# Layer 2 of a three-stage kernel: two operands of the activation put into PSUM, block sums read from SBUF, every transfer issued by one queue, loads issued earlier

## The chip, the cores and the metric

The kernel runs on one core of a Trainium2 chip. The metric is device microseconds of one execution, from repeated timed runs; a separate profiled execution gives the trace. The engines are named as in the profile: PE (matmuls), PEld (its weight loads), DVE (VectorE), ACT (ScalarE), POOL (GpSimd) and SP, which here only issues transfers. A name with a q at its end (ACTq, SPq) is the engine's sequencer.

## The reference, cut to what matters

An attention stage feeds a first two-matrix layer, and that one a second. All the changed code is in the second layer. With 1792 tokens, width 768 and inner width 2048:

```python
h = x @ w_in                                   # 1792x768 @ 768x2048
P = a[0] + a[1]*h + a[2]*h**2 + a[3]*h**3
Q = 1.0 + abs(b[0])*abs(h) + abs(b[1])*h**2
g = P / (Q + 1e-06)
out = g @ w_out                                # 1792x2048 @ 2048x768
```

## The kernel before, in words

**Precision.** Every matmul operand is split into a high and a low part, and a product is three matmuls (high by high, high by low, low by high). `split`, `split2`, `split_x` and `split_g2` are such splits: ACT casts the high part, and DVE (POOL where `nc.gpsimd` is named) subtracts it for the low part.

**Layer 2, first product.** The tokens are cut into four blocks of 512, 384, 512 and 384, taken in the order 0, 2, 1, 3. For each block there are 8 turns, so 32 turns `n` in all (`HN`). `first2(n)` runs 36 matmuls on PE and leaves two banks of h side by side, in one of the three PSUM tiles `hps` (turn 0 uses the two banks `hb`). So in turns 0 to 15 a step of the activation has 2 x 512 = 1024 elements for each partition, and in turns 16 to 31 it has 2 x 384 = 768.

**The activation.** `act_step(n)` does `act_a(n)` and then `act_b(n-1)`, one turn late. In `act_a`, ACT makes |h| (L733), b1|h|+b0 (L734) and a3 h + a2 (L736); POOL multiplies the second by the first, which gives q (L737); DVE builds the numerator u in two steps (L739, L741), and the second of them is the last reader of the `hps` tile, so that PE may use it for turn n+3. In `act_b`, ACT takes the logarithm of q + 1 (L750) and the exponential of its negative (L751), which is a first value r of 1/Q. DVE then makes (q+1) r (L752), (u+a0) r (L753) and the Newton product, ((q+1) r - 2) u (L754). All tensors of these three steps lie in SBUF, in tiles of one large buffer `sb`, handed out by two rings: `us` with four tiles for u, `aq` with six for |h|, q and r.

**Block sums.** The second product is a seven-product block scheme (two halves of the tokens by two halves of the inner width). It wants g's blocks "11", "12", "22" and four sums S1 to S4. `g_out(n)` stores a turn's g to the DRAM tensor `gk`. Once the four blocks of one place are there, `gs_load` loads them all again, POOL makes four sums (`gs_sums`, L818), and `gs_out` stores the four sums. Ten of the sixteen groups of sums are made in turns 15 to 31, and six during the second product. `wt_load`, `wt_sums` (POOL, L790) and `wt_out` do the like for w_out, in turns 5 to 12.

**Layer 2, second product.** `second2(u)` runs 112 units of 12 matmuls (9 for the narrower part), 1176 matmuls in all. Unit `u` needs g split (`split_g2(u)`) and every other unit a new piece of w_out split (`split_w2(v)`); `load_g2` and `load_w2` fetch them ahead. `evict` empties the banks (`obank`).

**Queues.** The program is written out in order, and each engine runs its own instructions in that order. A transfer whose data or buffer isn't ready holds back whatever stands behind it in the queue of the engine that issues it. Stores of g, and loads and stores of g's sums, are issued by ACT here, between its activations; so are the first eight loads of w_out (L864). The other transfers are issued by SP.

Of the kernel before, what the change touches and what calls it, by code (L numbers as in the profile page):

```python
# [11 lines left out]
F32 = mybir.dt.float32  # L12
# [29 lines left out]
def attention_moe_moe(ctx: ExitStack, tc: tile.TileContext, q, k, v, w_in1, w_out1, w_in2, w_out2, a, b2, out):  # L42
# [699 lines left out]

    gst = {}

    def act_b(n):
# [12 lines left out]
        gst[n] = (gk[p][:, at_ : at_ + 2, c0 : c0 + w], u_, u)  # L758
# [16 lines left out]

    def wt_load(kk):
        wsum[kk] = [wif.get(), wif.get()]
        for t, c in zip(wsum[kk], (kk, kk + HF)):
            nc.sync.dma_start(out=t, in_=wd[1][c]["o"])

    def wt_sums(kk):
        t, u = wsum[kk]
        b11, b12, b21, b22 = t[:, :HM], t[:, HM:], u[:, :HM], u[:, HM:]
        for o, i0, i1, op in (
            (b22, b22, b12, ALU.subtract),
            (b12, b12, b11, ALU.subtract),
            (b11, b22, b11, ALU.add),
            (b21, b11, b21, ALU.subtract),
        ):
            nc.gpsimd.tensor_tensor(out=o, in0=i0, in1=i1, op=op)  # L790

    def wt_out(kk):
        for i, t in enumerate(wsum[kk]):
            nc.sync.dma_start(out=wt[kk][i], in_=t)
            wif.put(t)

    hf = Ring([])
    gsum = {}

    def halves(part, kk):  # L800
        w = blocks[part][1]
        return [t[:, : 2 * w].rearrange("p (k t) -> p k t", k=2) for t in gsum[part, kk]]

    def gs_load(part, kk):
        c0, w = blocks[part]
        gsum[part, kk] = (hf.get(), hf.get())
        for i, t in enumerate(halves(part, kk)):
            nc.scalar.dma_start(out=t, in_=gk[kk][:, 2 * i : 2 * i + 2, c0 : c0 + w])

    def gs_sums(part, kk):  # L810
        g22, g21, g11, g12 = (t[:, i] for t in halves(part, kk) for i in range(2))
# [8 lines left out]
    def gs_out(part, kk):  # L820
        c0, w = blocks[part]
        for i, t in enumerate(halves(part, kk)):
            nc.scalar.dma_start(out=gk[kk][:, 4 + 2 * i : 6 + 2 * i, c0 : c0 + w], in_=t)
        hf.put(*gsum.pop((part, kk)))

# [119 lines left out]
    with tc.manual_schedule():  # L945
# [3 lines left out]

        hb.extend(fixed("hb", 2, [P, 512], F32, hb_p))  # L950
        pairs.put(*fixed("pair", 3, [P, 2, 512], F32, ps_p))
# [276 lines left out]
        def temps(w):  # L1228
            tm = [sb[:, i * 2 * w : (i + 1) * 2 * w] for i in range(10)]
            order_ = (0, 1, 2, 7, 8, 9, 3, 4, 5, 6) if w == BK else range(10)  # L1230
            tm = [tm[i] for i in order_]
            for ring, ts in ((us, tm[:4]), (aq, tm[4:])):
# [3 lines left out]
        temps(BK)
        SB2 = 20 * (BK - P)
        WTS = range(5, 13)
        GSUMS = {n: i for i, n in enumerate((15, 18, 20, 21, 23, 24, 26, 27, 29, 31))}
        GSUMS2 = {5 + 8 * i: 10 + i for i in range(6)}  # L1240
        GS = [(part, kk) for part in range(2) for kk in range(HF)]
        wt_held = []
        spare = []

        for n in range(HN):
            g, p = turn(n)
            nxt = turn(n + HF)[0] if n + HF < HN else None
            for kk in wt_held:
                wt_out(kk)
            wt_held.clear()  # L1250
            if n < 5:
# [3 lines left out]
                load_wi(2 * n + 12)  # L1255
            if n + 1 in WTS:
                wt_load(n + 1 - WTS[0])
            if n == WTS[-1] + 1:
                hf.put(*(wif_all[:, i * 2 * BK : (i + 1) * 2 * BK] for i in range(3)))
            if n == 2 * HF:  # L1260
                temps(BK - P)
            if n == 2 * HF + 3:
                hf.put(*(sb[:, SB2 + i * 2 * BK : SB2 + (i + 1) * 2 * BK] for i in range(3)))
            if nxt is not None and p in (3, 4, 5):
# [48 lines left out]
        obank.extend([*hb, *(hps[i % 3][:, j, :] for i in (1, 2, 0) for j in range(2))])  # L1313
        for u in range(NU):
            split_g2(u + 6)
            if u == 0:
                for i in range(9, 12):
                    load_g2(i)
            load_g2(u + 12)
            if u % 2 == 0:  # L1320
                load_w2(u // 2 + HF)
                if u >= 4:
                    split_w2(u // 2 + HF - 2)
            second2(u)
            if u == 1:
                act_step(HN)
            if u in (3, 6):
                g_out(HN - 3 + u // 3)
            if u == 2:
                gs_out(*GS[GSUMS[HN - 1]])  # L1330
                hf.free.clear()
                hf.put(*(wif_all[:, i * 2 * BK : (i + 1) * 2 * BK] for i in (2, 0, 1)))
                hf.put(sb[:, SB2 + 4 * BK : SB2 + 6 * BK])
            if u - 5 in GSUMS2:
                gs_out(*GS[GSUMS2[u - 5]])
            if u + 3 in GSUMS2:
                gs_load(*GS[GSUMS2[u + 3]])
            if u in GSUMS2:
                gs_sums(*GS[GSUMS2[u]])
# [34 lines left out]
```

## Time and profile before

| what | value |
|---|---|
| median of 3 runs | 1121.83 us (1117.86 to 1125.58) |
| the profiled execution's own time | 1126.82 us |
| its span, first to last instruction | 1125.0 us |
| mean granted PE clock | 0.979 of full |
| first matmul of layer 2 (L708) | 615.5 us into the span (its weight load) |
| last matmul (L888) starts | 1120.2 us |
| PE / DVE / ACT / POOL busy | 1065.1 / 843.9 / 605.5 / 306.3 us |

The trace is of one execution, whose own time lies 1.82 us above its span and 5.0 us above the median of the three runs. A busy PE is not a PE at its peak, because matmuls overlap in the records; the step from one start to the next tells the pace.

### The profile page before, as it was taken

What the parts mean: (1) busy time and instruction counts of PE and PEld (TensorE: products, weight loads), DVE (VectorE), ACT (ScalarE), POOL (GpSimd) and SP (SyncE); (2) the same over time, 40 slices, a digit from 0 to 9 for tenths busy, and PEclk for the clock granted to TensorE, in tenths of its full rate; (3) what the DMA queues carried; (4) which work ended last, traced back from release to release, by engine and by line L of the source; (5) the groups of instructions that cost most, each with busy time, mean ns of one, the idle gap of its engine ahead of it and who ended that gap; (6) DMA issues with size and microseconds to landing.
All of it is one profiled execution on the core that took longest, in us unless ns stands there. A gap on an engine that the chain in (4) does not pass through costs nothing.

```text
span 1125.0 us, 16087 instructions
## 1 busy us (share of the span) xinstructions
PE 1065.1 (95%) x5654; PEld 925.8 (82%) x5654; DVE 843.9 (75%) x1081; ACT 605.5 (54%) x911; POOL 306.3 (27%) x206
## 2 busy tenths in 40 slices
PE   9999999999999999999998999969977877999998
PEld 5555559999999999999997888859876877899997
DVE  4779777888877576858567499999997986556661
ACT  6778885566655543333224667565755554354340
POOL 2332200000000000000022749985777953210000
PEclk9999999999999999999999999989988988999999
DMA  8999866877667886979695435663678579986671
GB/s 244 287 269 266 241 229 218 280 257 238 209 232 252 277 283 219 320 248 348 213 332 209 125 128 188 226 209 134 234 238 274 188 257 296 297 272 217 189 230 50
DMA packets 157536, 265.02 MB, mean 236 GB/s; under 512 B 14096, under 2 KB 111888, under 8 KB 157456
## 3 DMA queue, kind: packets, MB, share of 16 engines
q1 hardware_dynamic: 117904, 196.85, 54.5%
q10 hardware_dynamic: 39488, 67.15, 17.6%
q8 instruction: 44, 0.72, 0.3%
q14 instruction: 36, 0.29, 0.1%
q0 software_dynamic: 64, 0.00, 0.0%
HBM read 174.69 MB, written 89.26 MB: 235 GB/s over the span
## 4 chain that ended last, share of the span: by engine, by line
PE 62%; DVE 12%; POOL 9%; DMA 7%; issue 5%; ACT 3%; ACTq 1%; SPq 0%; DVEq 0%; POOLq 0%
PE acc L501 13%; PE hp L888 10%; PE hb L342 5%; PE pair L318 5%; PE hb L501 5%; PE acc L638 4%; PE acc L639 4%; PE acc L637 4%; POOL wif L790 4%; PE hb L888 3%; POOL sb L737 2%; POOL wif L818 2%; DVE sb L753 2%; PE hb L637 2%; PE hb L639 2%
## 5 line engine op out<-in xcount | busy, mean ns | idle before, releaser
L370 POOL TENSOR_TENSOR w<-wif,w 128x768 fp32r<-128x768 f32 x2 | 3.9, 1973 | 424.5 <-ACT w L369 423.9
L333 ACT ACTIVATE sb<-pair,nls 128x896 f32<-128x896 f32 x84 | 81.0, 1009 | 32.9 <-PE pair L318 32.9
L638 PE MATMUL acc<-xa_all,woH 128*128 128x448 f32 x252 | 92.8, 368 | 4.9 <-DVE xa_all L366 4.9
L637 PE MATMUL acc<-xa_all,woH 128*128 128x448 f32 x252 | 92.5, 367 | 0.0
L639 PE MATMUL acc<-xa_all,woL 128*128 128x448 f32 x252 | 92.5, 367 | 0.0
L737 POOL TENSOR_TENSOR sb<-sb 128x1024 f32<-128x1024 f32 (+1 forms) x32 | 76.7, 2397 | 53.4 <-ACT sb L734 52.3
L708 PE MATMUL hp<-xa_all,woH 128*128 128x512 f32 (+1 forms) x168 | 64.2, 382 | 17.9 <-DVE sb L741 17.9
L342 PE MATMUL hb<-sb,vs 128*64 128x448 f32 (+1 forms) x384 | 73.9, 554 | 0.0
L501 PE MATMUL acc<-xb,wr 128*128 128x448 f32 x315 | 67.7, 366 | 0.0
L190 ACT ACTIVATE sb<-sb 128x768 f32<-128x768 f32 x64 | 57.9, 904 | 17.5 <-DVE xa_all L366 7.6
L196 DVE SCALAR_TENSOR_TENSOR sb<-sb 128x768 int32<-128x768 int32 x64 | 65.5, 1023 | 2.2
L818 POOL TENSOR_TENSOR wif<-wif 128x512 f32<-128x512 f32 (+1 forms) x34 | 50.1, 1474 | 62.4 <-DMA wif<-gk 61.0
L365 ACT CAST xa_all<-sb 128x448 fp32r<-128x448 f32 x67 | 37.7, 565 | 53.9 <-PE acc L639 21.4
L193 DVE SCALAR_TENSOR_TENSOR sb<-sb 128x768 int32<-128x768 int32 x64 | 64.9, 1014 | 2.2
L708 PE MATMUL hp<-hx,woH 128*128 128x512 f32 (+1 forms) x168 | 61.9, 368 | 3.0 <-DVE sb L741 3.0
L501 PEld LDWEIGHTS acc<-xb,wr 128*128 128x128 f32 x315 | 59.1, 188 | 5.4 <-issue 0.7
L709 PE MATMUL hp<-xa_all,woH 128*128 128x512 f32 (+1 forms) x168 | 63.2, 376 | 0.0
L710 PE MATMUL hp<-xa_all,woL 128*128 128x512 f32 (+1 forms) x168 | 63.1, 375 | 0.0
L710 PE MATMUL hp<-hx,woL 128*128 128x512 f32 (+1 forms) x168 | 61.5, 366 | 0.0
L709 PE MATMUL hp<-hx,woH 128*128 128x512 f32 (+1 forms) x168 | 61.5, 366 | 0.0
L754 DVE SCALAR_TENSOR_TENSOR sb<-sb 128x1024 f32<-128x1024 f32 (+1 forms) x32 | 60.3, 1884 | 1.1
L753 DVE SCALAR_TENSOR_TENSOR sb<-sb,nab 128x1024 f32<-128x1024 f32 (+1 forms) x32 | 59.5, 1860 | 0.0
(211 smaller groups left out, 2867.7 us busy)
## 6 DMA issues: line engine op xcount, KB each, us to landing
sb<-in_moe_w_in_dram SPq DMA_DIRECT2D x32, 768.0 KB, 7.3
sb<-in_moe_w_out_dram SPq DMA_DIRECT2D x32, 768.0 KB, 6.5
gd<-sb SPq DMA_DIRECT2D x64, 224.0 KB, 3.2
sb<-gd ACTq DMA_DIRECT2D x64, 224.0 KB, 5.4
wf<-w0i SPq DMA_DIRECT2D x32, 384.0 KB, 3.7
gk<-sb ACTq DMA_DIRECT2D x22, 512.0 KB, 3.0
gk<-sb ACTq DMA_DIRECT2D x22, 384.0 KB, 2.7
xs<-sb SPq DMA_DIRECT2D x36, 224.0 KB, 2.8
```

What stands on the lines that cost most here:

```text
L333: nc.scalar.activation(t, p[:, :, :S], AF.Sigmoid, bias=nls, scale=QKSCALE)
L342: nc.tensor.matmul(hb[i_ % 2][j * D : (j + 1) * D, :S], vs[i_][part, j, c * D : (c + 1) * D], t[part, j], start=(c == 0), stop=(c == LAST),)
L501: nc.tensor.matmul(o, w_[:, w], x[:, i_, :], start=first and kk == 0 and n_ == 0, stop=kk == HK - 1 and n_ == 2, skip_group_check=not first,)
L637: nc.tensor.matmul(o, woH[c][:, w], x[:, 0, :], start=(c == 0), stop=False)
L638: nc.tensor.matmul(o, woH[c][:, w], x[:, 1, :], start=False, stop=False)
L639: nc.tensor.matmul(o, woL[c][:, w], x[:, 0, :], start=False, stop=(c == KF - 1))
L708: nc.tensor.matmul(o, wh[:, w], x[:, 0, :wd_], start=first, stop=False)
L709: nc.tensor.matmul(o, wh[:, w], x[:, 1, :wd_], start=False, stop=False)
L710: nc.tensor.matmul(o, wl[:, w], x[:, 0, :wd_], start=False, stop=last)
L737: nc.gpsimd.tensor_tensor(out=q_, in0=q_, in1=a_, op=ALU.mult)
L753: nc.vector.scalar_tensor_tensor(out=u_, in0=u_, scalar=A0, in1=a_, op0=ALU.add, op1=ALU.mult)
L888: nc.tensor.matmul(o, a_, y[:, w_, :], start=kk == 0 and n_ == 0, stop=kk == HF - 1 and n_ == 2)
```

## The change

- `act_b`: the exponential r goes into `hpair`, which is the two PSUM banks `hb` made into one tile, and so does (q+1) r, which takes r's place there. The order of the first two DVE steps is exchanged: u is multiplied by r first, since r is then overwritten. There is one such pair of banks for all turns. `aq` shrinks from six tiles to four, and the tiles left over become buffers of the sums.
- Sums of g: for turns 8 to 15 and 24 to 29 (`SUMMED`) the sums are made two turns later from the turn's g while it is still in SBUF, so that only the other two blocks are loaded, and of g's two halves only one is stored. Turns 30 and 31 keep the old way, in the second product (`LATE`).
- Sums of w_out: four stay in turns 5 to 8, four move to turns 19, 21, 23 and 25.
- All transfers of the loop and of the second product are issued by SP.
- Loads: `load_w2` for the first eight pieces moves to turns 20 to 23, the first g loads to turn 22, later ones follow their splits at once; the splits run five units ahead (`LEAD`, six before).
- `obank`: the banks `hb` come last in the list, not first.

```diff
     def act_b(n):
...
+        r_ = hpair[0][:, :, :w]
         nc.scalar.activation(a_, q_, AF.Ln, bias=lnb[:, 0:1], scale=2.0**-63)
-        nc.scalar.activation(a_, a_, AF.Exp, bias=lnb[:, 1:2], scale=-1.0)
-        nc.vector.scalar_tensor_tensor(out=q_, in0=q_, scalar=ONE, in1=a_, op0=ALU.add, op1=ALU.mult)
-        nc.vector.scalar_tensor_tensor(out=u_, in0=u_, scalar=A0, in1=a_, op0=ALU.add, op1=ALU.mult)
-        nc.vector.scalar_tensor_tensor(out=u_, in0=q_, scalar=2.0, in1=u_, op0=ALU.subtract, op1=ALU.mult)
+        nc.scalar.activation(r_, a_, AF.Exp, bias=lnb[:, 1:2], scale=-1.0)
+        nc.vector.scalar_tensor_tensor(out=u_, in0=u_, scalar=A0, in1=r_, op0=ALU.add, op1=ALU.mult)
+        nc.vector.scalar_tensor_tensor(out=r_, in0=q_, scalar=ONE, in1=r_, op0=ALU.add, op1=ALU.mult)
+        nc.vector.scalar_tensor_tensor(out=u_, in0=r_, scalar=2.0, in1=u_, op0=ALU.subtract, op1=ALU.mult)
...
     def g_out(n):
         if n in gst:
-            dst, src, u = gst.pop(n)
-            nc.scalar.dma_start(out=dst, in_=src)
+            dst, src, u, _ = gst.pop(n)
+            nc.sync.dma_start(out=dst, in_=src)
...
+    def gs_sums(n, both=False):
+        w = blocks[turn(n)[0]][1]
+        x, y = (pair_of(t, w) for t in gsum[n])
+        g = y if both else gst[n][3]
         for o, i0, i1, op in (
-            (g22, g21, g22, ALU.add),
-            (g21, g11, g21, ALU.subtract),
-            (g11, g22, g11, ALU.subtract),
-            (g12, g12, g11, ALU.subtract),
+            (y[:, 0], g[:, 1], g[:, 0], ALU.add),
+            (y[:, 1], x[:, 0], g[:, 1], ALU.subtract),
+            (x[:, 0], y[:, 0], x[:, 0], ALU.subtract),
+            (x[:, 1], x[:, 1], x[:, 0], ALU.subtract),
         ):
             nc.gpsimd.tensor_tensor(out=o, in0=i0, in1=i1, op=op)
...
+        WTS = {**{5 + i: i for i in range(4)}, **{19 + 2 * i: 4 + i for i in range(4)}}
+        LEAD = 5
...
+            if 2 * HF + 4 <= n < 3 * HF:
+                for i in range(2):
+                    load_w2(2 * (n - 2 * HF - 4) + i)
...
             first2(n)
             act_step(n)
             if n in WTS:
-                wt_sums(n - WTS[0])
-                wt_held.append(n - WTS[0])
+                wt_sums(WTS[n])
+            if n - 2 in SUMMED:
+                gs_sums(n - 2)
             g_out(n - 2)
...
+            if n - 1 in WTS:
+                wt_out(WTS[n - 1])
+            if n - 3 in SUMMED:
+                gs_out(n - 3)
+            if n + 1 in WTS:
+                wt_load(WTS[n + 1], wif if n < HF else hf)
+            if n - 1 in SUMMED:
+                gs_load(n - 1)
...
+        obank.extend([*(hps[i % 3][:, j, :] for i in (1, 2, 0) for j in range(2)), *hb])
+        LATE = {22: HN - 2, 36: HN - 1}
         for u in range(NU):
-            split_g2(u + 6)
...
+            split_g2(u + LEAD)
+            load_g2(u + LEAD + 9)
+            for v in (u + HF - 3,) if u < 3 else (u // 2 + HF - 2,) if u >= 4 and u % 2 == 0 else ():
+                if not u:
+                    load_w2(v + HF - 1)
+                split_w2(v)
+                load_w2(v + HF)
```

What stands on ACT's queue from turn 25 of the kernel before (`hp0` is the tile of that turn; `gk7` is the store of turn 23's g, the L823 rows store sums, the L808 row loads blocks for sums, and eight L864 loads follow):

```order
L733 ACTIVATE sb_60<-hp0_5416 128x768
L734 ACTIVATE sb_60<-sb_60,absb_228 128x768
L736 ACTIVATE sb_60<-hp0_5416,nab_229 128x768
L750 ACTIVATE sb_60<-sb_60,lnb_230 128x768
L751 ACTIVATE sb_60<-sb_60,lnb_230 128x768
L763 DMA gk7_208<-sb_60 128x2x384
L823 DMA gk5_206<-wif_4119 128x2x512
L823 DMA gk5_206<-sb_60 128x2x512
L808 DMA sb_60<-gk6_207 128x2x512 x2
L864 DMA w03_1992<-w1o0_170 128x384
...
L365 CAST woL3_3719<-w03_1992 128x384
L853 CAST hx0_4113<-xa_all_234 128x512
```

And ACT's queue from the same turn of the changed kernel, up to the activations of the next:

```order
L734 ACTIVATE sb_60<-hp0_5415 128x768
L735 ACTIVATE sb_60<-sb_60,absb_228 128x768
L737 ACTIVATE sb_60<-hp0_5415,nab_229 128x768
L753 ACTIVATE sb_60<-sb_60,lnb_230 128x768
L754 ACTIVATE hb_291<-sb_60,lnb_230 128x2x384
L365 CAST w00_1988<-wif_4118 128x384
L734 ACTIVATE sb_60<-hp1_5416 128x768
```

The transfers are gone from ACT's queue, and the last activation of the turn writes the PSUM pair `hb` and no longer `sb`.

What stands on SP's queue of the changed kernel in turns 26 and 27 (L861 loads g for the second product, L767 stores a turn's g, L801 stores sums of w_out, L815 loads blocks for sums, L837 stores sums, L878 loads a piece of w_out):

```order
L861 DMA woL3_3718<-gk6_207 128x512
L861 DMA woH3_3717<-gk7_208 128x512
L861 DMA woL2_3716<-gk0_201 128x384
L767 DMA gk0_201<-sb_60 128x384
L801 DMA wt7_0_223<-sb_60 128x768
L801 DMA wt7_1_224<-sb_60 128x768
L815 DMA sb_60<-gk1_202 128x2x384
L878 DMA wif_4118<-w1o8_186 128x384
L861 DMA xa_all_234<-gk1_202 128x384
L767 DMA gk1_202<-sb_60 128x384
L837 DMA gk0_201<-sb_60 128x2x384 x2
L815 DMA sb_60<-gk2_203 128x2x384
```

In the kernel before, SP's queue holds only loads there (this is its part from the last x loads to the sixth g load):

```order
L675 DMA xa_all_234<-xs1_5_72 128x384
L847 DMA xa_all_234<-gk0_201 128x512
L847 DMA xa_all_234<-gk1_202 128x512
L847 DMA xa_all_234<-gk2_203 128x512
L847 DMA xa_all_234<-gk3_204 128x512
L847 DMA woL5_3723<-gk4_205 128x512
L847 DMA woH5_3722<-gk5_206 128x512
```

So loads that stood alone now stand between stores that wait for DVE (L767) and for POOL (L837, L801).

POOL's queue in turns 26 and 27 of the kernel before (L737 is the product q, L366 a split of w_out, L818 a group of sums):

```order
L737 TENSOR_TENSOR sb_60<-sb_60 128x768
L818 TENSOR_TENSOR sb_60<-sb_60 128x512 x4
L366 TENSOR_TENSOR woH3_3718<-w03_1992,woH3_3718 128x384
L366 TENSOR_TENSOR woL2_3717<-w02_1991,woL2_3717 128x384
L737 TENSOR_TENSOR sb_60<-sb_60 128x768
L818 TENSOR_TENSOR wif_4119<-wif_4119 128x512 x4
```

And of the changed kernel, from the end of turn 25 (L796 is a group of sums of w_out) to turn 27:

```order
L796 TENSOR_TENSOR sb_60<-sb_60 128x384 x4
L366 TENSOR_TENSOR w00_1988<-wif_4118,w00_1988 128x384
L738 TENSOR_TENSOR sb_60<-sb_60 128x768
L829 TENSOR_TENSOR sb_60<-sb_60 128x384 x4
L366 TENSOR_TENSOR woL5_3722<-wif_4118,woL5_3722 128x384
L738 TENSOR_TENSOR sb_60<-sb_60 128x768
L829 TENSOR_TENSOR sb_60<-sb_60 128x384 x4
```

The sums of g are narrower there (384 for 512), and one group of them stands in every turn from 26 on.

## Rows read from the trace of the kernel before

**Rows 1.** Busy time by stage: length, PE, PEld, DVE, ACT, POOL, PEclk, DMA share, GB/s.
```profile
615.70:740.00 124.30, 124.30 (x541) 101.25 (x539) 105.53 (x68) 77.88 (x81) 98.82 (x50) 1.00 0.51 176
740.00:891.00 151.00, 120.85 (x615) 115.69 (x615) 138.46 (x102) 94.11 (x112) 110.24 (x61) 0.91 0.63 216
891.00:965.00 74.00, 57.79 (x294) 56.04 (x293) 56.49 (x66) 35.20 (x65) 33.70 (x26) 0.88 0.80 264
965.00:1120.60 155.60, 154.17 (x884) 152.95 (x882) 85.22 (x157) 56.53 (x117) 12.03 (x11) 1.00 0.65 205
```
**Rows 2.** Waits of PE in layer 2: us in total, times, longest.
```profile
PE hp L708 <- DVE sb L741: 30.2, 11, 6.9
PE hp L888 <- ACT sb L903: 6.1, 1, 6.1
PE hb L888 <- DVE hx L854: 4.1, 1, 4.1
PE hp L888 <- DVE sb L387: 3.6, 3, 2.8
PE hb L888 <- DVE xa_all L854: 3.1, 1, 3.1
```
**Rows 3.** Timeline of PE: start us, us; starts 36 matmuls apart, for both widths.
```profile
623.85 0.40 PE L708 MATMUL hp<-hx,woH 128*128 128x512 f32 x1
...
632.25 0.40 PE L708 MATMUL hp<-hx,woH 128*128 128x512 f32 x1
...
767.65 0.34 PE L708 MATMUL hp<-hx,woH 128*128 128x384 f32 x1
...
774.01 0.34 PE L708 MATMUL hp<-hx,woH 128*128 128x384 f32 x1
```
**Rows 4.** Busy time in 20 us of the second product, columns as in Rows 1.
```profile
1000.00:1020.00 20.00, 20.00 (x117) 20.00 (x116) 12.66 (x22) 11.44 (x25) 2.84 (x3) 1.00 0.70 227
```
**Rows 5.** DVE's groups by form, 615.7 to 912 us: count | busy, mean ns | idle before.
```profile
L754 DVE SCALAR_TENSOR_TENSOR sb<-sb 128x1024 f32<-128x1024 f32 x16 | 35.5, 2219 | 0.6
L752 DVE SCALAR_TENSOR_TENSOR sb<-sb 128x1024 f32<-128x1024 f32 x16 | 32.6, 2038 | 0.0
L753 DVE SCALAR_TENSOR_TENSOR sb<-sb,nab 128x1024 f32<-128x1024 f32 x16 | 30.7, 1920 | 0.0
L753 DVE SCALAR_TENSOR_TENSOR sb<-sb,nab 128x768 f32<-128x768 f32 x15 | 27.8, 1853 | 0.0
L754 DVE SCALAR_TENSOR_TENSOR sb<-sb 128x768 f32<-128x768 f32 x15 | 23.8, 1589 | 0.5
L752 DVE SCALAR_TENSOR_TENSOR sb<-sb 128x768 f32<-128x768 f32 x15 | 21.3, 1423 | 0.0
L741 DVE SCALAR_TENSOR_TENSOR sb<-sb,nab,hp 128x1024 f32<-128x1024 f32 x15 | 19.2, 1281 | 0.5
L739 DVE TENSOR_TENSOR sb<-hp,sb 128x1024 f32<-128x1024 f32 x15 | 18.2, 1214 | 9.0 <-ACT sb L736 9.0
L741 DVE SCALAR_TENSOR_TENSOR sb<-sb,nab,hp 128x768 f32<-128x768 f32 x16 | 16.2, 1015 | 0.6
L739 DVE TENSOR_TENSOR sb<-hp,sb 128x768 f32<-128x768 f32 x16 | 15.2, 947 | 5.6 <-ACT sb L736 5.6
```
**Rows 6.** Timelines of POOL and of DVE near 843 us: start us, us.
```profile
842.22 1.82 POOL L737 TENSOR_TENSOR sb<-sb 128x768 f32<-128x768 f32 x1
...
842.94 1.92 DVE L752 SCALAR_TENSOR_TENSOR sb<-sb 128x768 f32<-128x768 f32 x1
```
**Rows 7.** Timeline of ACT near 853 us: eight transfers issued, nothing else.
```profile
853.21 5.04 ACTq L864 DMA_DIRECT2D w<-w1o  x8
```
**Rows 8.** POOL's sums of width 384 by form, as in Rows 5.
```profile
L818 POOL TENSOR_TENSOR sb<-sb 128x384 f32<-128x384 f32 x5 | 7.3, 1456 | 0.3
...
L818 POOL TENSOR_TENSOR wif<-wif 128x384 f32<-128x384 f32 x1 | 1.0, 1006 | 0.0
```
**Rows 9.** A wait of ACT in the first product's second half.
```profile
ACT hx L681 <- DMA xa_all<-xs: 12.0, 1, 12.0
```

More of the change, by code (lines that the diff above doesn't have):

```diff
@@ L686, in attention_moe_moe @@
     hps = {}
+    hpair = []
     def turn(n):
@@ L743, in attention_moe_moe @@
     gst = {}
+    SUMMED = [*range(HF, 2 * HF), *range(3 * HF, 4 * HF - 2)]
     def act_b(n):
@@ L792, in wt_out @@
     def wt_out(kk):
-        for i, t in enumerate(wsum[kk]):
+        ring, ts = wsum.pop(kk)
+        for i, t in enumerate(ts):
             nc.sync.dma_start(out=wt[kk][i], in_=t)
-            wif.put(t)
-    hf = Ring([])
+            give_back(ring, t)
     gsum = {}
[L800 to L808, printed above, removed]
@@ L810, in gs_sums, with pair_of, gs_load @@
-    def gs_sums(part, kk):
-        g22, g21, g11, g12 = (t[:, i] for t in halves(part, kk) for i in range(2))
+    def pair_of(t, w):
+        return t[:, : 2 * w].rearrange("p (k t) -> p k t", k=2)
+    def gs_load(n, both=False):
+        g, kk = turn(n)
+        c0, w = blocks[g]
+        c0 %= NH
+        x, y = hf.get(), hf.get()
+        gsum[n] = (x, y)
+        nc.sync.dma_start(out=pair_of(x, w), in_=gk[kk][:, 2:4, c0 : c0 + w])
+        if both:
+            nc.sync.dma_start(out=pair_of(y, w), in_=gk[kk][:, 0:2, c0 : c0 + w])
@@ L817, in gs_sums, with gs_out @@
         ):
             nc.gpsimd.tensor_tensor(out=o, in0=i0, in1=i1, op=op)
[L820 to L824, printed above, removed]
+    def gs_out(n):
+        g, kk = turn(n)
+        c0, w = blocks[g]
+        c0 %= NH
+        x, y = gsum.pop(n)
+        for at_, t in ((4, y), (6, x)):
+            nc.sync.dma_start(out=gk[kk][:, at_ : at_ + 2, c0 : c0 + w], in_=pair_of(t, w))
+            give_back(hf, t)
@@ L948, in attention_moe_moe @@
         ps_p, ps_s = opened("ps", space=PSUM)
-        hb.extend(fixed("hb", 2, [P, 512], F32, hb_p))
+        hb_all = hb_p.tile([P, 2, 512], F32, tag="hb", name="hb")
+        hb.extend(hb_all[:, j] for j in range(2))
+        hpair.append(hb_all)
         pairs.put(*fixed("pair", 3, [P, 2, 512], F32, ps_p))
@@ L1228, in temps @@
         def temps(w):
[L1229 to L1232, printed above, removed]
+            tm = [sb[:, i * 2 * w : (i + 1) * 2 * w] for i in range(sum(sizes) // (2 * w))]
+            if w == BK:
+                tm.insert(3, tm.pop(7))
+            for ring, ts in ((us, tm[:4]), (aq, tm[4:8])):
                 ring.free.clear()
                 ring.put(*ts)
[L1236 to L1242, printed above, removed]
+            return tm[8:]
+        rest = temps(BK)
+        WTS = {**{5 + i: i for i in range(4)}, **{19 + 2 * i: 4 + i for i in range(4)}}
+        LEAD = 5
         spare = []
@@ L1255, in attention_moe_moe @@
                 load_wi(2 * n + 12)
[L1256 to L1259, printed above, removed]
+            if n == HF + 1:
+                hf.put(*rest, *(wif_all[:, i * 2 * BK : (i + 1) * 2 * BK] for i in range(3)))
             if n == 2 * HF:
-                temps(BK - P)
-            if n == 2 * HF + 3:
-                hf.put(*(sb[:, SB2 + i * 2 * BK : SB2 + (i + 1) * 2 * BK] for i in range(3)))
+                rest = temps(BK - P)
+            if n == 2 * HF + 2:
+                hf.free.clear()
+                hf.put(*rest[4:], *rest[:4])
             if nxt is not None and p in (3, 4, 5):
@@ L1270, in attention_moe_moe @@
                         load_x(nxt, d)
-            if n == 3 * HF:
+            if n == 2 * HF + 4:
+                wsrc.put(*(wif_all[:, i * HM : (i + 1) * HM] for i in range(8)))
+            if 2 * HF + 4 <= n < 3 * HF:
+                for i in range(2):
+                    load_w2(2 * (n - 2 * HF - 4) + i)
+            if n == 3 * HF - 2:
                 gsrc.put(*xin.free)
@@ L1329, in attention_moe_moe @@
             if u == 2:
-                gs_out(*GS[GSUMS[HN - 1]])
+                gs_out(HN - 3)
                 hf.free.clear()
[L1332 to L1339, printed above, removed]
+                hf.put(*rest[4:])
+            if u - 4 in LATE:
+                gs_out(LATE[u - 4])
+            if u + 3 in LATE:
+                gs_load(LATE[u + 3], True)
+            if u in LATE:
+                gs_sums(LATE[u], True)
             for _ in range(2):
```

58 lines of the change are left out of this document (18 added, 40 removed).

## The prediction

> **What bounds the kernel now.** I read the stages first [rows 1]. Up to 615.7 us the changed code plays no part. The two products of layer 2 then take 124.3 + 151.0 = 275.3 us (32 turns, to 891) and 74.0 + 155.6 = 229.6 us (1176 matmuls). The next view is PE's own pace. Where nothing holds it, 36 matmuls of width 512 take 632.25 - 623.85 = 8.40 us, and of width 384 774.01 - 767.65 = 6.36 us [rows 3]; in the second product 117 matmuls go in 20 us, 0.171 each [rows 4]. At this pace the first product would take 16 x 8.40 + 16 x 6.36 = 236.2 us and the second 1176 x 0.171 = 201.0 us. So 39.1 and 28.6 us are lost, together 67.7 us, and no more than this can come back.
>
> Where they go is in PE's waits [rows 2]: 30.2 us for L741, DVE's last reading of the `hps` tile, and in the second product 6.1 + 4.1 + 3.6 + 3.1 = 16.9 us for ACT's evictions and for DVE. The other 8.9 and 11.7 us I put down to a slower clock and to restarts: the granted clock is 1.00 up to 740, 0.91 in the stretch after and 0.88 from 891 to 965 [rows 1], and it is below full only where PE has been idle.
>
> Why L741 is late is in DVE's groups [rows 5]. A turn of width 1024 costs DVE 1.21 + 1.28 + 2.04 + 1.92 + 2.22 = 8.67 us, more than PE's 8.40; of width 768 it costs 0.95 + 1.02 + 1.42 + 1.85 + 1.59 = 6.83, more than PE's 6.36, and the splits come on top. DVE is busy 138.5 of the 151 us there. It is the bound of the first product, and it enters the second with a backlog. The reader is to see that the five steps have equal sizes, yet the two that read a PSUM bank take 1.21 and 1.28 us and the three with both inputs in `sb` take 1.92 to 2.22, and only these vary. One case shows why: L752 starts at 842.94 while POOL is in L737 until 844.04, and ends 0.82 us after it [rows 6]. It waited for POOL to finish.
>
> **The three DVE steps.** After the change each has one input in PSUM and one in `sb`, as L739 and L741 have now, so I price them by these: 0.95 to 1.02 us at 768 and 1.21 to 1.28 at 1024 [rows 5]. A turn then costs DVE 1.21 + 1.28 + 3 x 1.25 = 6.2 us and 0.95 + 1.02 + 3 x 0.98 = 4.9 us, which is 2.2 and 1.4 us less than PE's turn. The other end of this price is what the steps cost today, for an output in PSUM (the new (q+1) r) has no row here; I take the low end, because a PSUM operand is what the rows at the low end have in common.
> The Trainium skill speaks of this in "SBUF — State Buffer", section "Who interferes with whom": a DVE instruction with two SBUF inputs and a POOL instruction that reads SBUF exclude each other for the length of the one that started first, and with at most one SBUF input (outside the two-port modes) DVE is not held up. By that rule the three steps run free and the sum stays; if only the rows' duration for `sb` inputs held, the first product would keep its 275 us. The trace agrees: none of the L739 and L741 groups is slowed.
> POOL gains by the same: its steps no longer wait for these three.
>
> **One pair of banks, four `aq` tiles.** The exponential of turn n-1 must wait for the Newton step of turn n-2, and L734 of turn n for the product with q of turn n-2. Both are done by DVE before it begins turn n, and DVE begins that only after ACT's L736 of turn n. At 4.9 us of 6.36 DVE is through in time, so the price is nothing; if DVE lagged, ACT would be tied to it.
>
> **ACT without transfers.** Eight transfers alone kept ACT's sequencer for 5.04 us [rows 7], and the next cast stood behind them; ACT is busy only 94 of the 151 us [rows 1], so what it loses are such waits. They become SP's, where an issue costs no more than the same 0.63 us: six a turn make 3.8 of 6.36 us, so SP keeps up. What is queued behind a waiting store on SP are loads. This has a row now: ACT waited 12.0 us for a load of x [rows 9] that stood behind stores of w_out's sums. Afterwards the loads of g and w_out are issued 9 and up to 16 units before they are needed (9 units of at least 9 matmuls at 0.171 us are 14 us), and the sums' blocks a turn and a half before.
>
> **Sums and loads.** POOL's product takes 1.82 us [rows 6] and a sum of width 384 1.01 us when free, 1.46 when held [rows 8]. In turns 26 to 31 POOL does one product, four sums and in five of them a split, which I price as a sum: 1.82 + 5 x 1.01 = 6.9 us against 6.36. It falls behind by 0.5 us a turn, 3 in all, and its product is not wanted until the turn after: no cost on the path. The wide sums are in turns with 8.40 us. In the second product 2 groups of sums remain of 6, so less traffic and fewer waits of ACT in the stretch with a DMA share of 0.80 [rows 1].
>
> **The sum.** First product: of 30.2 us of waits I leave 4 (the x loads of turns 4, 12 and 20, and DVE's splits, which still exclude POOL), and of 8.9 us of slow clock 1.5. Second product: of 16.9 us I leave 5 (the first units start while DVE and ACT finish turns 30 and 31; output buffers), and of 11.7 us 4. Bounds of these four remainders are 0 and the present values. Gain 26.2 + 7.4 + 11.9 + 7.7 = 53.2 us. The profiled execution's own time, 1126.82 us (span 1125.0 and 1.82 around it), becomes 1073.6. It lies 4.99 us above the median of the three runs; in the same ratio the median 1121.83 becomes 1068.9, and I say 1068.
>
> **Rivals.**
> - *POOL becomes the bound at the end of the first product.* Against DVE's remaining splits, and with sums at 1.46 us, a turn of POOL costs 1.82 + 5 x 1.46 = 9.1 us, 2.8 more than PE's, 16 to 17 us over six turns. About a turn of that (6.4) is absorbed by the three `hps` tiles; 10 us reach PE, with 4 us of slow clock behind them: 1068 + 14 = 1082. For it: one group of sums in each of these turns, in order ahead of the next product. Against it: the three DVE steps that held the sums up are gone.
> - *The three steps stay slow*, because what holds them is not the second `sb` input, or because writing to PSUM costs as much. Then the change doesn't do what it says, the first product keeps its loss but for ACT's waits (some 5 us), and the second's 20 us come back: 1126.8 - 25 = 1102, in the median's measure 1097.
> - *SP's queue becomes the bound; slower than before.* Stores that wait for POOL (16 groups of sums, 8 of w_out) hold back loads that PE needs, as in [rows 9]. The gain of 53 and 1% (11 us) are gone if each of the 14 groups in the loop costs PE 4.6 us. At 5.4 us each the time is 1068 + 76 = 1144. For it: the stores wait for POOL's end of a turn. Against it: the loads' lead.
>
> **How the numbers follow.** Forecast 0.62, POOL 0.22, steps stay slow 0.11, SP 0.05. If all that is lost came back, the time would be 1126.82 - 67.7 = 1059.1, in the median's measure 1054; with the spread of the runs I set the low end at 1053. The high end, 1094, takes in POOL's case with half as much again, and leaves out the last two (0.16) and a little at either end. What a measurement of this kernel can tell from no change is about 1%, 1110.6 to 1133.0. Forecast, POOL and nearly all of the third case are faster; SP's case, mostly, is slower: 0.93, 0.03, 0.04.
>
> **What the changed profile would show.** L755 to L757, the three DVE steps of `act_b`: 0.95 to 1.02 us at 768 whatever POOL does. PE's waits for `hps` under 8 us in all. A first product of 236 to 246 us and a second of 201 to 212. A granted clock near 1.00 from 740 to 965. No transfer on ACT's sequencer between 620 us and the last store. Wrong it would be if the three steps kept 1.4 us or more, if POOL's group of sums in turns 26 to 31 took over 6 us, or if SP waited on POOL while ACT waited on a load.

## The result and the profile after

The changed kernel took 1073.8 us, the median of 4 runs (1072.28 to 1078.69), against 1121.16 us for the kernel before, the median of its 4 (1117.86 to 1125.58). The ratio is 0.9583, with a 95% interval of 0.9537 to 0.9628. The forecast was 1068 us in a range of 1053 to 1094.

The profiled execution is the longest of the four, 1078.69 us with a span of 1076.9. First come its stages, cut where the products of layer 2 begin, with the columns of [rows 1].

```profile
623.40:740.00 116.60, 116.60 (x508) 95.15 (x508) 80.47 (x72) 83.28 (x88) 80.38 (x50) 1.00 0.51 172
740.00:856.50 116.50, 116.50 (x647) 113.77 (x646) 104.08 (x101) 88.07 (x104) 94.29 (x71) 1.00 0.81 272
856.50:930.00 73.50, 66.76 (x367) 64.56 (x366) 51.01 (x81) 41.41 (x82) 23.70 (x20) 0.98 0.81 263
930.00:1072.50 142.50, 141.64 (x813) 140.71 (x811) 72.53 (x142) 50.42 (x102) 4.06 (x4) 1.00 0.56 176
```

In both rows of the first product PE's busy time (the second figure) equals the length, and the granted clock (third from the end) is 1.00. PE doesn't stop once in 233.1 us, from 623.4 to 856.5, where it needed 275.3 before. DVE is busy 104.1 of 116.5 us in the second row, so it has room; in [rows 1] it had 138.5 of 151. The second product takes 215.9 us, from 856.5 to 1072.4, where it needed 229.6. Layer 2 begins 7.8 us later than in the kernel before: its first matmul starts at 623.44 us, there at 615.69. The three differences, 42.2 + 13.7 - 7.8 = 48.1 us, are the difference of the two spans.

The rows of layer 2 in the view of PE's waits answer to [rows 2]:

```profile
PE hp L902 <- POOL woH L366: 2.7, 1, 2.7
PE hp L902 <- ACT hx L867: 1.8, 2, 1.3
PE hp L902 <- DVE woL L366: 1.1, 1, 1.1
PE hp L902 <- DVE sb L742: 1.0, 1, 1.0
PE hb L902 <- DVE sb L387: 0.8, 2, 0.7
PE hb L902 <- ACT sb L917: 0.2, 1, 0.2
```

They add up to 7.6 us, where [rows 2] had 47.1. The wait of 30.2 us for DVE's last reading of `hps` (L741 before, L742 now) is 1.0 us. The longest one left is new: PE waits for POOL, which makes the low part of a piece of w_out (`woH` is only the tile in which the piece now lies).

Next DVE's groups by form, from 615 us to the end, with the columns of [rows 5].

```profile
L755 DVE SCALAR_TENSOR_TENSOR sb<-sb,nab,hb 128x1024 f32<-128x1024 f32 x16 | 20.4, 1276 | 0.2 <-ACT hb L754 0.2
L757 DVE SCALAR_TENSOR_TENSOR sb<-hb,sb 128x1024 f32<-128x1024 f32 x16 | 19.6, 1224 | 0.5
L756 DVE SCALAR_TENSOR_TENSOR hb<-sb,hb 128x1024 f32<-128x1024 f32 x16 | 19.5, 1221 | 0.0
...
L740 DVE TENSOR_TENSOR sb<-hp,sb 128x1024 f32<-128x1024 f32 x15 | 18.3, 1223 | 26.2 <-ACT sb L737 26.2
...
L755 DVE SCALAR_TENSOR_TENSOR sb<-sb,nab,hb 128x768 f32<-128x768 f32 x16 | 16.1, 1008 | 1.5 <-ACT hb L754 1.5
L757 DVE SCALAR_TENSOR_TENSOR sb<-hb,sb 128x768 f32<-128x768 f32 x16 | 15.3, 957 | 0.6
L756 DVE SCALAR_TENSOR_TENSOR hb<-sb,hb 128x768 f32<-128x768 f32 x16 | 15.3, 954 | 0.0
L740 DVE TENSOR_TENSOR sb<-hp,sb 128x768 f32<-128x768 f32 x16 | 15.3, 954 | 8.8 <-ACT sb L737 8.7
```

The three steps of `act_b` went from 2.04, 1.92 and 2.22 us to 1.28, 1.22 and 1.22 at 1024, and from 1.42, 1.85 and 1.59 to 1.01, 0.95 and 0.96 at 768. DVE now waits 26.2 us for ACT in the wide turns, where it waited 9.0 [rows 5]: it has become the engine that waits.

POOL's groups in the same stretch, its product (L738) and its sums of g (L829), narrow forms:

```profile
L829 POOL TENSOR_TENSOR sb<-sb 128x384 f32<-128x384 f32 x32 | 35.0, 1101 | 54.3 <-DMA sb<-gk 52.9
L738 POOL TENSOR_TENSOR sb<-sb 128x768 f32<-128x768 f32 x16 | 30.9, 1929 | 9.5 <-ACT sb L735 9.4
```

A sum of width 384 fell from 1.46 us [rows 8] to 1.10. POOL gained as well.

### The profile page after: what moved, and what is told of

Read it like the earlier page. It is cut to its first block, busy times and chain, and to the rows that moved or that the text cites. A ratio compares the mean times of both kernels' runs of the same rounds, so it can differ in the third digit from the quotient of the medians.

```text
span 1076.9 us, 16129 instructions
## 1 busy us (share of the span) xinstructions
PE 1056.9 (98%) x5654; PEld 916.2 (85%) x5654; DVE 767.0 (71%) x1084; ACT 605.3 (56%) x911; POOL 250.4 (23%) x203
## 4 chain that ended last, share of the span: by engine, by line
PE 75%; DVE 13%; ACT 4%; DMA 3%; issue 3%; POOL 1%; SPq 1%; ACTq 0%; DVEq 0%; POOLq 0%
PE acc L501 13%; PE hp L902 12%; PE hb L342 6%; PE pair L318 6%; PE hb L501 5%; PE hb L902 4%; PE acc L638 4%; PE acc L639 4%; PE acc L637 4%; PE hp L710 3%; PE hp L709 3%; PE hp L711 3%; PE hb L637 2%; PE hb L639 2%; PE hb L638 2%
## 5 line engine op out<-in xcount | busy, mean ns | idle before, releaser
L637 PE MATMUL acc<-xa_all,woH 128*128 128x448 f32 x252 | 93.1, 369 | 0.0
L738 POOL TENSOR_TENSOR sb<-sb 128x1024 f32<-128x1024 f32 (+1 forms) x32 | 70.8, 2213 | 41.8 <-ACT sb L735 41.7
L342 PE MATMUL hb<-sb,vs 128*64 128x448 f32 (+1 forms) x384 | 73.9, 554 | 0.3 <-DVE xk L355 0.3
L501 PE MATMUL acc<-xb,wr 128*128 128x448 f32 x315 | 68.6, 368 | 0.0
L193 DVE SCALAR_TENSOR_TENSOR sb<-sb 128x768 int32<-128x768 int32 x64 | 63.8, 997 | 2.2
L196 DVE SCALAR_TENSOR_TENSOR sb<-sb 128x768 int32<-128x768 int32 x64 | 63.4, 991 | 2.2
L501 PEld LDWEIGHTS acc<-xb,wr 128*128 128x128 f32 x315 | 59.0, 188 | 6.3 <-issue 0.7
L829 POOL TENSOR_TENSOR sb<-sb 128x384 f32<-128x384 f32 (+1 forms) x43 | 49.5, 1159 | 54.7 <-DMA sb<-gk 52.9
L709 PE MATMUL hp<-xa_all,woH 128*128 128x512 f32 (+1 forms) x168 | 60.7, 362 | 0.0
L711 PE MATMUL hp<-xa_all,woL 128*128 128x512 f32 (+1 forms) x168 | 60.7, 362 | 0.0
L710 PE MATMUL hp<-xa_all,woH 128*128 128x512 f32 (+1 forms) x168 | 60.7, 362 | 0.0
L740 DVE TENSOR_TENSOR sb<-hp,sb 128x768 f32<-128x768 f32 (+1 forms) x31 | 33.6, 1084 | 35.0 <-ACT sb L737 34.9
L318 PEld LDWEIGHTS pair<-xa_all 64*128 64x128 f32 x384 | 34.7, 190 | 24.9 <-issue 12.3
## 6 DMA issues: line engine op xcount, KB each, us to landing
gd<-sb SPq DMA_DIRECT2D x64, 224.0 KB, 3.1
sb<-gd ACTq DMA_DIRECT2D x64, 224.0 KB, 4.7
xs<-sb SPq DMA_DIRECT2D x36, 224.0 KB, 2.8
```

What stands on the lines that cost most here:

```text
L318: nc.tensor.matmul(p[:, j, :S], K[rows[j], a_, c * P : (c + 1) * P], Q[rows[j], b_, :], start=(n == 0), stop=(n == len(turns) - 1),)
L342: nc.tensor.matmul(hb[i_ % 2][j * D : (j + 1) * D, :S], vs[i_][part, j, c * D : (c + 1) * D], t[part, j], start=(c == 0), stop=(c == LAST),)
L501: nc.tensor.matmul(o, w_[:, w], x[:, i_, :], start=first and kk == 0 and n_ == 0, stop=kk == HK - 1 and n_ == 2, skip_group_check=not first,)
L637: nc.tensor.matmul(o, woH[c][:, w], x[:, 0, :], start=(c == 0), stop=False)
L709: nc.tensor.matmul(o, wh[:, w], x[:, 0, :wd_], start=first, stop=False)
L710: nc.tensor.matmul(o, wh[:, w], x[:, 1, :wd_], start=False, stop=False)
```

## Experiments

Each ratio is taken against the kernel before, run beside it on the same chip.

**PSUM taken away from the change.** The exponential and (q+1) r go back to SBUF; all the rest of the change stays.

```
-        r_ = hpair[0][:, :, :w]
+        r_ = a_
```

> The changed kernel with the exponential and (q+1) r put back into SBUF; all else stays. Theory 'lock' (the three steps were slow because two SBUF inputs must wait for POOL): L755 to L757 go back to means of 1.3 to 2 us, DVE's turn exceeds PE's again at width 768, PE's waits for the first product come back to 10 us or more, and the time is 1085 to 1105 us. Theory 'queue' (ACT without transfers made the gain): under 1079 us, PE's waits in the first product stay below 3 us.

Measured: 1168.7 us, ratio 1.0397 (1.0371 to 1.0422). It is slower than the kernel before, so the first theory is right about the steps and wrong about the size. In DVE's groups from 618 to 940 us the steps are held again:

```profile
L756 DVE SCALAR_TENSOR_TENSOR sb<-sb 128x1024 f32<-128x1024 f32 x16 | 32.6, 2039 | 1.8
L757 DVE SCALAR_TENSOR_TENSOR sb<-sb 128x1024 f32<-128x1024 f32 x16 | 32.2, 2013 | 0.6
L755 DVE SCALAR_TENSOR_TENSOR sb<-sb,nab 128x1024 f32<-128x1024 f32 x16 | 27.8, 1736 | 0.2 <-ACT sb L754 0.2
...
L740 DVE TENSOR_TENSOR sb<-hp,sb 128x1024 f32<-128x1024 f32 x15 | 18.4, 1225 | 47.3 <-ACT sb L737 47.3
```

Yet they are no slower than before, and still the first product takes 319.5 us. The longest waits of all engines in that stretch show what came on top:

```profile
ACT sb L734 <- DVE sb L757: 138.6, 28, 7.2
POOL sb L738 <- ACT sb L735: 98.1, 29, 7.5
DVE sb L740 <- ACT sb L737: 91.9, 30, 11.3
```

ACT waits for DVE and DVE for ACT: a circle. A turn's first step needs an `aq` tile, the change has four of these where there were six, and DVE's last step is what frees one. PE stands 51 us for it in the first product.

**Four `aq` tiles in the kernel before**, the rival explanation put to the test. At the change of width two tiles of turn 15 are overwritten by turn 16, so the output isn't the reference's.

```
-            for ring, ts in ((us, tm[:4]), (aq, tm[4:])):
+            for ring, ts in ((us, tm[:4]), (aq, tm[4:8])):
```

> The kernel before with four tiles for the exponential and the product with q in place of six, and nothing else. It is to tell why the change with r in SBUF was slower than the kernel before. If with four tiles ACT can begin a turn only after DVE's last step of the turn before the last, and DVE then waits for ACT in turn, so that the two work one after the other wherever DVE is the slower: 1140 to 1175 us, with ACT's first step waiting over 80 us in all for DVE. If the cause was another (sums in each of the last eight turns, all transfers on one queue), it stays at 1118 to 1130.

Measured: 1151.17 us, ratio 1.0239 (1.0211 to 1.0267). The waits from 613 to 930 us:

```profile
POOL sb L737 <- ACT sb L734: 83.8, 23, 8.2
DVE sb L739 <- ACT sb L736: 67.2, 29, 10.1
ACT sb L733 <- DVE sb L753: 65.4, 21, 6.8
PE hp L708 <- DVE sb L741: 44.5, 19, 8.1
```

The circle is there with nothing but the tiles changed: ACT waits 65.4 us with its first step and, in another row of the view, 19.6 us with its second, 85 in all (the expectation had put over 80 on the first alone). So four tiles cost 27 us where DVE is slow. In the change, where PE doesn't stop in the first product, they cost nothing, because the PSUM part made DVE fast. The two parts can't be priced apart and then added. The tiles don't explain all of the run before: it was 45 us slower than the kernel before, and where the other 18 lie was not traced.

**PSUM alone.** The kernel before, with the two operands in PSUM, one tile for the two banks, and the order of the banks that follows from it.

```
-        nc.scalar.activation(a_, a_, AF.Exp, bias=lnb[:, 1:2], scale=-1.0)
+        r_ = hpair[0][:, :, :w]
+        nc.scalar.activation(r_, a_, AF.Exp, bias=lnb[:, 1:2], scale=-1.0)
...
+        hb_all = hb_p.tile([P, 2, 512], F32, tag="hb", name="hb")
...
-        obank.extend([*hb, *(hps[i % 3][:, j, :] for i in (1, 2, 0) for j in range(2))])
+        obank.extend([*(hps[i % 3][:, j, :] for i in (1, 2, 0) for j in range(2)), *hb])
```

> The kernel before with the exponential and (q+1) r in PSUM alone (and the bank order that this needs in the second product). Theory 'lock': L752 to L754 take 0.95 to 1.02 us at width 768, the first product falls from 275 to about 245 us, the time is 1085 to 1098 us. Theory 'queue': ACT still issues transfers, the time stays above 1108 us.

Measured: 1089.32 us, ratio 0.9704 (0.967 to 0.9738), as expected. PSUM alone gives 33 of the 47 us. Its stages:

```profile
615.40:740.00 124.60, 124.60 (x543) 101.78 (x543) 85.44 (x78) 89.08 (x94) 85.20 (x56) 1.00 0.59 201
740.00:855.00 115.00, 109.30 (x613) 107.00 (x611) 90.35 (x93) 81.17 (x98) 80.41 (x56) 1.00 0.75 256
855.00:930.00 75.00, 62.96 (x328) 61.84 (x329) 54.04 (x68) 37.48 (x69) 32.44 (x27) 0.89 0.84 279
930.00:1079.00 149.00, 148.07 (x850) 146.96 (x848) 82.44 (x153) 54.84 (x114) 8.65 (x8) 1.00 0.65 205
```

Against the change the first product takes 239.6 us for 233.1, and the second 224.0 for 215.9. PE stands 5.7 us in the second row and 12.0 in the third, where the clock is 0.89; in the change these rows have 0 and 6.7.

**PSUM alone, without the late groups of sums.**

```
+        if GS_ALL.index((part, kk)) >= 10:
+            return
```

> The kernel before with the exponential and the product (q+1)r in PSUM, and of the six groups of sums in its second product the loads and POOL's sums left out (what is stored there are old blocks, so the result is another). It is to tell where the 15 us lie that PSUM alone does not give. If these late groups are it, by their bytes and POOL's share in the stretch with the DMA share near 0.9, the time falls by 6 to 10 us, to 1079 to 1084 us, and ACT waits less for loads of w_out in the second product. If the order of loads and splits is it, the time stays at 1087 to 1091 us.

Measured: 1081.81 us, ratio 0.9625 (0.9586 to 0.9664), 7.5 us less. The six late groups, of which the change keeps two, hold about half of the 15 us. The two intervals only just part. The second half of the expectation failed: ACT waits no less for w_out (16.3 and 5.3 us for `wt`, by the tile written, between 850 and 960, where it was 13.9 and 6.4). Which wait the groups caused, and where the other 7 us lie, these runs leave open.

**POOL's sums left out of the kernel before.** If POOL holds DVE, it must show without touching DVE's steps.

```
-        ):
+        )[:0]:
```

(in `wt_sums` and in `gs_sums`, so that the loop over the sums is empty)

> The kernel before without POOL's sums of blocks, of g and of w_out (their loads and stores stay, the blocks go back unsummed, so the result is another). If POOL's instructions hold up the three DVE steps whose inputs are both in SBUF, one product a turn is left to do it: half or more of the hold of 2.4 us in a wide turn goes, a turn of DVE falls from 8.67 to 7.4 us or less, under PE's 8.40, and the time to 1088 to 1108 us; the three steps get means near 1.6 us at 1024 and 1.25 at 768. If the three steps are slow by themselves, whatever POOL does, they keep 1.92 to 2.22 us and the time stays at 1115 to 1125.

Measured: 1096.58 us, ratio 0.9756 (0.9721 to 0.979). DVE's groups, 616 to 890 us:

```profile
L754 DVE SCALAR_TENSOR_TENSOR sb<-sb 128x1024 f32<-128x1024 f32 x16 | 35.2, 2202 | 0.6
L753 DVE SCALAR_TENSOR_TENSOR sb<-sb,nab 128x1024 f32<-128x1024 f32 x16 | 27.4, 1712 | 0.0
L752 DVE SCALAR_TENSOR_TENSOR sb<-sb 128x1024 f32<-128x1024 f32 x16 | 24.0, 1501 | 0.0
L754 DVE SCALAR_TENSOR_TENSOR sb<-sb 128x768 f32<-128x768 f32 x15 | 20.5, 1367 | 0.5
```

L752, untouched, falls from 2.04 to 1.50 us at 1024. L754, which meets the product in 8 of its 16 turns, stays at 2.20. The three together fall from 6.18 to 5.41 us; in the change they are 3.72. The time went where expected, the steps less far than the 1.6 us that I gave as their mean (1.80), so that a turn of DVE is 7.9 us and not 7.4.

At 1024 these means alone don't show that POOL is the cause: the kernel before with four tiles keeps all of POOL's sums, and its three steps add up to 5.41 us as well. The trace of the kernel before shows it when the 96 instructions of the three steps are taken one by one. At 768, the 10 during which POOL has no TENSOR_TENSOR running take 0.94 to 1.01 us, and the 38 others 1.74 in the mean and up to 2.64. At 1024 it is 8 of 1.22 to 1.28 us, and 40 of 2.22 in the mean and up to 3.33. In the change 81 of the 96 overlap one of POOL's, and none takes more than 1.01 us at 768 or 1.28 at 1024. Over all the runs of L752 in this kernel the shortest is 949 ns, and L756 of the change, with an operand and its output in PSUM, has 951 ns as its shortest from 760 us on. So for these steps PSUM isn't faster; it is only out of POOL's way.

The Trainium skill, "SBUF — State Buffer", section "Who interferes with whom", has the rule: a DVE instruction with two SBUF inputs and a POOL instruction that reads SBUF exclude each other. The traces agree with it: 2.22 us in the mean beside POOL and 1.22 to 1.28 without it with two SBUF inputs, and at most 1.28 us beside POOL with one.

**The queue of ACT.** The change, with the stores of g and the loads and stores of its sums on ACT's queue again.

```
-            nc.sync.dma_start(out=dst, in_=src)
+            nc.scalar.dma_start(out=dst, in_=src)
```

(and so at the three other places, in `gs_load` and `gs_out`)

> The changed kernel with g's stores and the loads and stores of the sums issued by ACT again. Theory 'lock': ACT has slack in the first product (172 us busy of 234), so at most 6 us are lost, 1074 to 1080 us. Theory 'queue': ACT's waits come back and with them PE's, 1088 us or more.

Measured: 1074.17 us, ratio 0.9555 (0.953 to 0.958). That is the change's time. Which queue carries these transfers is worth nothing that can be measured here. The eight loads of w_out that [rows 7] shows on ACT's queue stayed on SP's, so their move is not tested by this.

**The old lead of w_out's loads.**

```
-                for v in ws[i - 1] if i else ():
-                    load_w2(v + HF)
...
-                if not u:
-                    load_w2(v + HF - 1)
                 split_w2(v)
-                load_w2(v + HF)
+            if u % 2 == 0:
+                load_w2(u // 2 + HF)
```

> The change with the loads of w_out in the second product issued as late as in the kernel before: two pieces ahead of their split, and none of the extra ones during the last turns of the first product. If the longer lead is what keeps ACT from waiting for loads, its casts wait as in the kernel before, PE stands some 5 to 10 us more in the second product, and the time is 1079 to 1086 us. If the loads come early enough with the old lead, since ACT's sequencer is free and fewer bytes are moved, it stays at 1072 to 1076 us.

Measured: 1075.28 us, ratio 0.9554 (0.9533 to 0.9575). No cost in the time, although ACT does wait for the loads, by its rows between 840 and 960 us:

```profile
ACT woH L365 <- DMA wif<-wt: 15.5, 5, 6.2
ACT woL L365 <- DMA wif<-wt: 11.8, 6, 4.0
```

The waits were forecast rightly, their price was not: PE stands 8.7 us in all in layer 2, against 7.6 in the change. Waits of ACT are no loss as long as a piece is still split before PE wants it.

**One tile for the two banks, alone.**

```
-        hb.extend(fixed("hb", 2, [P, 512], F32, hb_p))
+        hb_all = hb_p.tile([P, 2, 512], F32, tag="hb", name="hb")
+        hb.extend(hb_all[:, j] for j in range(2))
```

> The kernel before with the two banks hb made one tile and nothing else. The profile of the changed kernel reaches layer 2 7.8 us later than that of before. Theory 'chance' (the start of the clock and PE's pace differ between executions): the ratio is 1.000 within 0.004. Rival (the one tile makes PE wait for the other bank's readers): 1124 to 1129 us, ratio 1.003 to 1.007, and waits of PE on hb in layer 1.

Measured: 1128.67 us, ratio 1.0038 (1.0022 to 1.0055): about 4 us, in a line that carries no work. That lies in both of the expected ranges; what speaks against chance is that the interval leaves out 1.000, and that PE waits for `hb` in layer 1 (0.9 us at L637, 0.2 at L501), which it doesn't in the kernel before.

**The change with `hb` apart until layer 2**, the cure for this: two tiles, whose pool is closed after layer 1, and a pair in the pool of layer 2.

```
-        hb_all = hb_p.tile([P, 2, 512], F32, tag="hb", name="hb")
-        hb.extend(hb_all[:, j] for j in range(2))
-        hpair.append(hb_all)
+        hb.extend(fixed("hb", 2, [P, 512], F32, hb_p))
...
+        hb_s.close()
         ps_p = ctx.enter_context(tc.tile_pool(name="ps2", bufs=1, space=PSUM, reuse_waits="tile"))
+        hpair.extend(fixed("hr", 1, [P, 2, 512], F32, ps_p))
+        hb[:] = [hpair[0][:, j] for j in range(2)]
```

> The change with the two banks hb as two tiles up to the end of layer 1, and as one tile of two banks only from layer 2 on. If the one tile ties readers and writers of the two banks together in attention and layer 1, which the kernel before with this alone put at 4.3 us, the time is 1068 to 1071 us and layer 2 starts some 4 us sooner. If those 4 us were chance or belong to the clock, it stays at 1073 to 1075.

Measured: 1068.55 us, ratio 0.9504 (0.948 to 0.9527), 5 us less than the change (9 by the two ratios, whose intervals don't meet). Layer 2 begins at 616.2, 7.3 us sooner. Some 2.3 us of this can be seen at the very start. PE's busy time from 8 to 12 us, with count, granted clock, DMA share and GB/s, in the change and then in this kernel:

```profile
8.00:12.00 4.00, 4.00 (x18) 1.00 0.69 201
```

```profile
8.00:12.00 4.00, 4.00 (x30) 1.00 0.72 191
```

The reason is in the timeline of ACT, in the change and then with `hb` apart. Its first cast there reads k out of the first bank. With one tile it waits for L295, q's transposes into the second bank, and starts at 6.68 us; with two it waits only for L292, k's own, and starts at 5.81.

```profile
6.68 1.02 ACT L301 CAST xa_all<-hb 128x512 fp32r<-128x512 f32 x2 [1.74 <-PE hb L295]
```

```profile
5.81 0.59 ACT L301 CAST xa_all<-hb 128x512 fp32r<-128x512 f32 x1 [0.88 <-PE hb L292]
```

The timeline of PE in the change shows where that lands:

```profile
7.75 1.46 PE L318 MATMUL pair<-xa_all 64*128 64x448 f32 x4 [0.47 <-ACT xa_all L301]
...
10.80 1.12 PE L292 MATMUL pair<-ident,km 128*128 128x128 f32 x4
```

And in the kernel with `hb` apart:

```profile
9.73 0.66 PE L292 MATMUL pair<-ident,km 128*128 128x128 f32 x4
```

After the stop of 0.47 us four transposes take 1.12 us, and here 0.66. PE runs on at the slow pace for some 4 us more, and its first matmul of L342 starts at 14.81 us in place of 12.51. (The column of the granted clock says 1.00 in both rows from 8 to 12 us, so the pace is read from the instructions.) Waits for `hb` in layer 1 account for 1.3 us more (0.8 at L501 and 0.5 at L637 in the change). Most of the rest is a slightly lower pace without waits, 2.9 us between 179 and 345 us; the kernel before with one tile has at most 0.7 of it, so most of it is not shown to come from the tile.

The other profiles settle whether the tile does anything. In all eight with one tile ACT's first cast waits for L295, and in all five with two it waits for L292. The last matmul of L637 into `hb` starts at 553.3 to 557.8 us in the eight and at 550.4 to 552.8 in the five, 3.7 us apart in the means. The change's profile is the latest of all, so about half of its 7.8 us belongs to that execution, the longest of its four.

**The loop's splits of w_out on DVE.**

```
-                    split_w2(v, nc.gpsimd)
+                    split_w2(v)
```

> The change with the five splits of w_out in the loop on DVE in place of POOL. If POOL's backlog at the end of the first product is what PE waited for at 869 us (2.7 us, a split of w_out's high half on POOL), that wait goes with a little slow clock behind it: 1069 to 1073 us. If DVE, which has its own split held by POOL there, only takes over the lateness, the time stays at 1073 to 1077.

Measured: 1071.19 us, ratio 0.953 (0.9506 to 0.9554). The 2.7 us for POOL's split are gone from PE's waits. The time is 2.6 us under the change's, but its interval reaches into the change's.

**Both together.**

> The change with both: hb as two tiles up to the end of layer 1, and the five splits of w_out in the loop on DVE. If the two gains (5 us for hb apart, 2.6 us for the splits, each against the change) lie at different places, they add up: 1064 to 1068 us. If the gain of the splits on DVE was chance, the time stays at that of hb apart, 1067 to 1070 us.

Measured: 1066.52 us, ratio 0.9484 (0.9457 to 0.9511), with 5.6 us of waits of PE in layer 2. That is the lowest time of all. The gain by `hb` apart is told from the change (0.948 to 0.9527 against 0.9537 to 0.9628); what the splits on DVE add to it, 2 us in the medians, is not told from nothing.

## Why the prediction was right, and where its sizes were off

**The DVE steps.** Right, to the hundredth: 0.95 to 1.01 us at 768 whatever POOL does. The reason holds too: in the kernel before the steps are long only beside POOL's instructions, and putting r back in SBUF lengthens the steps again.

**First product.** Forecast 236.2 us of pace and 5.5 of remainders, 241.7; measured 233.1. The remainders (waits of 4, clock of 1.5) were 0. The pace was mis-sized by 3: I took one turn of each width from [rows 3], but the pace has two values per width. Starts of matmuls 36 apart in the change, in turns 3 and 10:

```profile
648.42 0.40 PE L709 MATMUL hp<-hx,woH 128*128 128x512 f32 x1
...
656.82 0.40 PE L709 MATMUL hp<-hx,woH 128*128 128x512 f32 x1
...
706.84 0.39 PE L709 MATMUL hp<-xa_all,woH 128*128 128x512 f32 x1
...
715.00 0.39 PE L709 MATMUL hp<-xa_all,woH 128*128 128x512 f32 x1
```

The first pair is 8.40 us apart, the second 8.16. Eight turns of each, and 6.36 and 6.24 at the other width, make 233.3. So 233.1 lies below the 236 to 246 that were to be a sign of being right.

**Second product.** Forecast 201.0 + 5 + 4 = 210; measured 215.9, beyond the 201 to 212 of the signs. Here too the pace was mis-sized by 3: the 117 matmuls in the 20 us of [rows 4] include two that only reach into the stretch. By their starts in the kernel before, 117 matmuls take 20.31 us, 0.174 each, and 1176 take 204.1:

```profile
1000.04 0.33 PE L888 MATMUL hp<-woL,xa_all 128*128 128x384 f32 x1
...
1020.35 0.33 PE L888 MATMUL hp<-woL,xa_all 128*128 128x384 f32 x1
```

Waits are 7.6 us instead of 5. What is left for clock and restarts is 4.2, as forecast. The gain by fewer groups of sums was right in direction (7.5 us for six late groups). The term "ACT without transfers" was not borne out as far as it was tested: ACT does gain a free sequencer, but with g's stores and the sums' transfers back on its queue the time is the same.

**Ahead of layer 2.** Forecast nothing, since I read the change as playing no part there. It does: the one tile for `hb` costs 4 to 5 us, by two experiments from opposite sides. This is the step of the prediction that failed, and it makes up most of the distance from 1068 to 1073.8: with `hb` apart the measured time is 1068.55. Part of that agreement is luck, as the first product was 8.6 us better than forecast and the second 5.9 worse. In the profiled execution 5.1 us are missing (1078.69 us for a forecast of 1073.6): 7.8 later into layer 2, 8.6 won, 5.9 lost.

**Four `aq` tiles.** Priced at nothing, "if DVE lagged, ACT would be tied to it". Both halves were shown: PE doesn't stop in the change's first product, and four tiles cost 27 us where DVE lags.

**The rivals.** POOL as the bound at the end was there as a mechanism and small in size, in the rows of POOL and of ACT near 869 us of the change:

```profile
868.08 0.99 POOL L366 TENSOR_TENSOR woH<-wif,woH 128x384 fp32r<-128x384 f32 x1
869.03 2.28 POOL L738 TENSOR_TENSOR sb<-sb 128x768 f32<-128x768 f32 x1
```

```profile
871.35 0.94 ACT L753 ACTIVATE sb<-sb,lnb 128x768 f32<-128x768 f32 x1 [3.55 <-POOL sb L738]
```

POOL comes to the last product late, ACT waits 3.55 us for it, and PE waits 2.7 us for the split ahead of it. That is 3 us where the rival said 14. Slow steps are refuted. The queue of SP as the bound is refuted as well: with most of the moved transfers back on ACT's queue nothing is gained, and no row of PE's waits in layer 2 names a load.

## What to carry to other kernels

When DVE steps of equal size take unequal times, look for POOL beside them before looking at DVE. Moving one operand to an idle PSUM bank gave at least as much as taking POOL's sums away altogether (a ratio of 0.970 against 0.976, with intervals that overlap), and the steps are no slower for it. A buffer that is taken away to pay for such a move costs nothing only as long as the move works, so price the two together. And merging two tiles into one merges their waits everywhere in the program, also in phases that the change wasn't meant to touch.

## What was not expected of the hardware

- In the change PE stopped for 0.47 us at 7.3 us of the program and kept the slow pace until about 13 us (transposes of 128 in 0.28 us each instead of 0.165); with `hb` apart it didn't stop and kept it until about 9. That the stop alone does this isn't shown: the kernel before with four `aq` tiles has no such stop, but 1.24 us of idle time just before 5.2 us, and kept the slow pace until about 11.
- Matmuls of one shape go at two paces without any wait: 8.40 and 8.16 us for 36 of width 512. In the change the slower pace is that of turns 1 to 7, with the moving operand in `hx`; but turn 0, with its weights in another tile, has it there too and takes 8.18 us, and at width 384 turn 21 of the kernel before, with the same tiles as turn 17, takes 6.24 us where that takes 6.36. So the tile alone doesn't decide, and what does wasn't tried.
